# Splits of the first y rows one expert step later, those of the next rows in two items, and double decodings in the odd items

## The chip, the cores and the metric

One NeuronCore of one Trainium2 chip runs the whole program. The time is the device time of one execution in microseconds (us); three runs of the kernel before are shown, and one further execution was profiled. The engines are TensorE (PE, with its weight loads as PEld), VectorE (DVE), ScalarE (ACT), GpSimd (POOL) and SyncE (SP), which here mainly issues DMAs.

## What is computed

Three layers follow each other: causal attention with a bias, a mixture of eight experts that sends each token to one expert, and a gated layer without routing. The change lies at the seam of the last two.

```python
# attention: 4 batches, 8 heads, 576 positions, head size 64
scores = scale * q @ k.T ; bias = min(-(cum_i - cum_j), 0) ; causal
x = softmax(scores + bias) @ v                     # 2304 tokens x 512
# experts: w1 512x1024, w2 1024x512, one of eight for each token
for e in range(8):
    h = np.maximum(x[mask] @ w1[e], 0.0)
    out[mask] = gate_w[mask, None] * (h @ w2[e])
# gated layer: w_a, w_b 512x1536, w_out 1536x512
out = (x @ w_a) * (x @ w_b) @ w_out
```

## The kernel before

**Precision by splitting.** Every matmul operand is held as a hi part and a lo part (hi is the value rounded to a shorter format, lo the rest), and each product takes three matmuls: hi by hi, lo by hi and hi by lo. So each operand costs a cast for hi, mostly on ACT, and a subtraction for lo, on DVE or POOL. In the rows, xh and xl, hh and hl are such pairs, and so are the two halves of a weight tile w, v or u.

**Weights of the gated layer.** They arrive as 64-bit numbers and have to be decoded. `vload` issues the DMA of half a weight into one of three staging buffers (st). `vsplit` decodes one half: ACT scales one word into cv (line 238), DVE shifts the other (239) and merges twice (246, 249). `vfinish` then makes hi on ACT (1207) and lo on POOL (1209) for the half that was decoded one step earlier. A **tick** is one `vload` and one `vsplit`. There are two cv buffers. 36 halves are needed in all: for each pair f, f+1 of twelve column groups a tile of w_a, one of w_b and one of w_out.

**Experts.** `hmm(e, f)` computes column group f (0 to 7) of the hidden layer, 12 matmuls into a PSUM bank h, from which ACT takes hh (1271) and DVE hl (1272). `ymm(e, f)` multiplies the group of one step earlier with w2, 12 matmuls into four banks y. After f = 7 the four y banks are copied to mx tiles (171, 173) and stored to the tensor yt in DRAM (1294), in rows sorted by expert.

**Gated layer.** Rows of yt are processed in six groups i of 384. `yload(i)` loads a group from yt into the one xg buffer (1305). `ysplit(i, d)`, d from 0 to 3, makes hi and lo of a quarter of it: xh on ACT (1312), then xl on DVE (1313). `abmm(i, f)` computes a = y w_a into bank h (12 matmuls, over d) and b = y w_b into bank x (12 more). ACT copies a into an mx tile (1331), DVE multiplies it with b (1333), ACT and DVE make hi and lo of the product (1334, 1335). For i < 2 bank h0 and bank x0 are single, so the next item's a waits for the copy and its b for the product. `omm` (nine matmuls of 512 columns, line 1343) follows one item later.

**Order.** In this part the order on each engine is the order in which the code is written. The last expert, e = 7, runs f = 0 to 7 with one tick in each step. Then come the items, numbered k from 0: (0,0), (0,1), (1,0), (1,1), and from there alternately i = 0 and 1 up to f = 11, item 23; after it groups 2 to 5, without ticks. In items 16 to 20 four small indirect DMAs each, `m6` on POOL (1248), write row numbers and weights to the tensor pm; they are loaded as pmt (1500) before the first output. `oout` scales an output bank by pmt (1352 on ACT, 1354 on DVE) and scatters it by an indirect DMA on POOL (1355).

Of the kernel before, what the change touches and what calls it, by code (L numbers as in the profile page):

```python
# [24 lines left out]
E = 8  # L25
# [7 lines left out]
TICKS = (1, 1, 2)  # L33
# [104 lines left out]
def moe_kernel(tc, q, k, v, s, emb, tau, w1, w2, wa, wb, wo, out, dbg=None):  # L138
# [6 lines left out]
    def pool(st, n, b, **kw):  # L145
        return st.enter_context(tc.tile_pool(name=n, bufs=b, **kw))
# [28 lines left out]
    with left, right:  # L175
# [96 lines left out]
        if True:  # L272
# [816 lines left out]
            def bank(nm, n=2):  # L1089
                turn[nm] = turn.get(nm, -1) + 1  # L1090
                return ps.tile([128, 512], F32, name="%s%d" % (nm, turn[nm] % n))
# [37 lines left out]
            def xtr(e, d):  # L1129
                if d == 0:  # L1130
                    xhs[e] = [xhp.tile([128, 4, GT], F32R, name=x)[:, :, :CAPS[e]] for x in ("xh", "xl")]
                xh, xl = xhs[e]
                cap = CAPS[e]
                pt = bank("x") if e else bank("y", 4)
                for a in range(3):
                    m = min(128, cap - 128 * a)
                    nc.tensor.transpose(  # L1137
                        out=pt[:, 128 * a:128 * a + m], in_=xgs[e][:m, a, 128 * d:128 * d + 128], identity=ident[:m, :m]
                    )
                nc.scalar.copy(out=xh[:, d, :], in_=pt[:, :cap])  # L1140
                nc.vector.tensor_tensor(out=xl[:, d, :], in0=pt[:, :cap], in1=xh[:, d, :].bitcast(F32), op=ALU.subtract)
# [37 lines left out]
            def vload():  # L1179
                if loaded2[0] < len(jobs2):  # L1180
                    key, h, src, _ = jobs2[loaded2[0]]
                    stg[key, h] = slot_load64(src)
                    loaded2[0] += 1
# [3 lines left out]
            def vsplit():  # L1187

                new = None
                if split2[0] < loaded2[0]:  # L1190
                    key, h, _, nm = jobs2[split2[0]]
                    t = stg.pop((key, h))
                    c = decode1(t)
                    new = (key, h, nm, c, split2[0])
                if half:
                    vfinish()
                if new:
                    decode2(t, c)
                    half.append(new)
                    split2[0] += 1  # L1200
# [57 lines left out]
            def hmm(e, f):  # L1258
                ph = bank("h")
                xh, xl = xhs[e]  # L1260
                k_ = 0
                for d in range(4):
                    w = slots[e, d]
                    for hl, mv in ((0, xh), (0, xl), (1, xh)):
                        nc.tensor.matmul(  # L1265
                            ph[:, :CAPS[e]], lhsT=w[:, hl, 128 * f:128 * f + 128], rhs=mv[:, d, :],
                            start=k_ == 0, stop=k_ == 11,
                        )
                        k_ += 1
                hh, hl_ = (hp.tile([128, GT], F32R, name=x)[:, :CAPS[e]] for x in ("hh", "hl"))  # L1270
                nc.scalar.activation(out=hh, in_=ph[:, :CAPS[e]], func=AF.Relu)
                nc.vector.scalar_tensor_tensor(
                    out=hl_, in0=ph[:, :CAPS[e]], scalar=0.0, in1=hh.bitcast(F32), op0=ALU.max, op1=ALU.subtract
                )
                hs[e, f] = (hh, hl_)

            def ymm(e, f):
                if f == 0:
                    ys[e] = [bank("y", 4) for d in range(4)]
                hh, hl_ = hs.pop((e, f))  # L1280
                w = slots[e, 4 + f // 2]
                c0 = 512 * (f % 2)
                for d in range(4):
                    for k_, (hl, mv) in enumerate(((0, hh), (0, hl_), (1, hh))):
                        nc.tensor.matmul(  # L1285
                            ys[e][d][:, :CAPS[e]], lhsT=w[:, hl, c0 + 128 * d:c0 + 128 * d + 128], rhs=mv,
                            start=f == 0 and k_ == 0, stop=f == 7 and k_ == 2,
                        )
                if f == 7:
                    br = nc.sync.value_load(ci[:1, 0, e:e + 1], min_val=max(0, N * (e - 1) // (E - 1)), max_val=N)  # L1290
                    for d in range(4):
                        yv = mxp.tile([128, 512], F32, name="mx")[:, :CAPS[e]]
                        copy("DA"[d % 2], yv, ys[e][d][:, :CAPS[e]])
                        nc.sync.dma_start(out=yt[:, d, bass.ds(br, CAPS[e])], in_=yv)

            def tick():
                vload()
                vsplit()
# [8 lines left out]
            def ysplit(i, d):  # L1307
                if d == 0:
                    yhs[i] = [xhp.tile([128, 4, GT], F32R, name=x) for x in ("xh", "xl")]
                yh, yl = yhs[i]  # L1310
                t = xgs[E + i][:, d, :]
                nc.scalar.copy(out=yh[:, d, :], in_=t)
                nc.vector.tensor_tensor(out=yl[:, d, :], in0=t, in1=yh[:, d, :].bitcast(F32), op=ALU.subtract)  # L1313
# [120 lines left out]
            for e in range(E):  # L1434
                if e == 1:
                    sched.close()
                    overflow()
                    sched.enter_context(tc.manual_schedule())
                for f in range(8):
                    hmm(e, f)  # L1440
                    if (e, f) == (0, 2):
                        most = nc.values_load(ci[:1, 2, 0:1], min_val=-CAP, max_val=N)
                    if prev:
                        ymm(*prev)
                    prev = (e, f)
                    if (e, f) == (0, 1):
                        xload(1)
                    if (e, f) == (1, 0) or f == 7 and 0 < e < E - 2:
                        xload(e + 2 - (f == 0))
                    if (e, f) == (E - 1, 1):  # L1450
                        yload(0)
                    if f == 4 and e + 2 < E:
                        zfill(e + 2)
                    if 3 <= f < 7:
                        if e + 1 < E:
                            xtr(e + 1, f - 3)
                        else:
                            ysplit(0, f - 3)
                    if e == E - 1 and f == 7:
                        yload(1)  # L1460
                    for _ in range(2 if (e, f) == (0, 1) else 1):
                        wsplit2()
                        wload2()
                    if e == E - 2 and f >= 6:
                        vload()
                    if e == E - 1:
                        for _ in range(TICKS[0]):
                            tick()
                    if misc and (e or f > 1):
                        misc.pop(0)()  # L1470

# [3 lines left out]
            for k_, (i, f) in enumerate(items):  # L1475
                abmm(i, f)
                if (i, f) == (NG - 1, 11):
                    for t, x in ((0, 10), (1, 10), (0, 11), (1, 11), (2, 10), (2, 11)):
                        omm1(i, x, t)
                        if x == 11:  # L1480
                            oout(i, t)
                elif k_:
                    omm(*prev)
                else:
                    for d in range(4):
                        ysplit(1, d)
                    ymm(*prev)
                    mo.close()
                    rto.close()
                    rings["u"] = pool(right, "ringc", 1, side="right")  # L1490
                prev = (i, f)
                for _ in range(TICKS[1] + (k_ % TICKS[2] == 0) if i < 2 else 0):
                    tick()
                if (i, f) == (1, 0):
                    yload(2)
                if 16 <= k_ < 21:
                    for t in range(4 * (k_ - 16), 4 * (k_ - 15)):
                        m6(t)
                if k_ == 21:
                    nc.sync.dma_start(out=pmt, in_=pm.rearrange("(t p) x -> p t x", p=128))  # L1500
                if (i, f) == (0, 11):
                    for d in range(4):
                        ysplit(2, d)
                if 1 < i < NG - 1:
                    if f == 1:
                        yload(i + 1)
                    if 4 <= f < 8:
                        ysplit(i + 1, f - 4)
# [34 lines left out]
```

## Time and profile before

| | us |
|---|---|
| runs shown | 986.53, 985.0, 986.75 (median 986.53) |
| profiled execution | 984.46 |
| its span | 982.5 |
| PE busy in it | 950.0 |
| DVE, ACT, POOL busy | 500.9, 425.4, 341.6 |

The span is the stretch that the profile covers; the 1.96 us between it and the execution's time lie outside the trace. Times in the rows below count from the span's start. The last expert runs from about 494 to 519, item 0 starts at 519.1 and item 24 at about 670. A busy time is summed over stages with different limits, so what a part of the code costs is read from the waits and the timeline of its stage.

### The profile page before, as it was taken

The numbers are of one execution on the slowest core, as the hardware profiler recorded it, in microseconds if no ns is written. First come the engines' busy times: TensorE is split into PE (matmuls) and PEld (weight loads), VectorE is DVE, ScalarE is ACT, GpSimd is POOL, SyncE is SP. The second block draws the span as 40 slices with busy tenths as digits, with TensorE's granted clock in tenths as the row PEclk, the third lists the DMA queues.
The fourth block names the chain that finished last, engine by engine and source line by source line (L and its number), as shares of the span: only waits on it lengthen the run. The fifth ranks groups of instructions, "written<-read, shape, count | busy, mean of one in ns | idle before, by whom it ended". The sixth has DMA issues, their size and how long they took to land.

```text
span 982.5 us, 17967 instructions
## 1 busy us (share of the span) xinstructions
PE 950.0 (97%) x6470; PEld 860.2 (88%) x6471; DVE 500.9 (51%) x1312; ACT 425.4 (43%) x1059; POOL 341.6 (35%) x488
## 2 busy tenths in 40 slices
PE   8999999999799999999999999999999999999996
PEld 6787777877589999999999999999999999999995
DVE  5678778787656334444478888723222222222111
ACT  4678777777645444454545444422111111111111
POOL 6665657569423333333333433562001001001001
PEclk8999999999899999999999999999999999999999
DMA  6877897887276766677565544303010010000000
GB/s 169 196 179 194 204 215 195 199 199 210 71 221 174 216 196 211 180 218 217 175 198 180 174 128 127 89 2 98 1 33 33 1 33 33 1 1 33 1 1 32
DMA packets 105413, 123.68 MB, mean 126 GB/s; under 512 B 56937, under 2 KB 71225, under 8 KB 105321
## 3 DMA queue, kind: packets, MB, share of 16 engines
q1 hardware_dynamic: 101433, 112.77, 42.2%
q0 software_dynamic: 3616, 9.48, 2.8%
q8 instruction: 52, 0.85, 0.4%
q14 instruction: 40, 0.33, 0.1%
q10 hardware_dynamic: 272, 0.26, 0.1%
HBM read 86.04 MB, written 19.92 MB: 108 GB/s over the span
## 4 chain that ended last, share of the span: by engine, by line
issue 32%; PE 27%; DVE 3%; POOL 3%; DMA 2%; ACT 0%; POOLq 0%; SPq 0%; DVEq 0%; ACTq 0%
PE h L1265 9%; PE y L1285 9%; PE h L1325 3%; PE x L1325 3%; PE y L1343 2%; POOL out_dram L1355 1%; DMA pm<-pd,pos 1%; DVE cv L246 1%; POOL pm L1248 1%; DVE cv L249 1%; PE x L1137 1%; DMA st<-in_moe_w_b_dram 1%; PE x L1343 0%; PE h L1343 0%; DVE xl L1313 0%
## 5 line engine op out<-in xcount | busy, mean ns | idle before, releaser
L1333 DVE TENSOR_TENSOR mx<-x,mx 128x384 f32<-128x384 f32 x72 | 40.0, 555 | 228.8 <-PE x L1325 228.7
L1355 POOL DMA_INDIRECT out_dram<-mx,pmt x18 | 17.7, 984 | 292.2 <-DVE mx L1354 288.5
L599 ACT ACTIVATE z<-z,mn 128x576 f32<-128x576 f32 (+4 forms) x160 | 89.6, 560 | 48.9 <-DVE mn L593 47.9
L1334 ACT CAST hh<-mx 128x384 fp32r<-128x384 f32 x72 | 36.9, 512 | 163.4 <-DVE mx L1333 163.4
L523 POOL TENSOR_SCALAR bt<-ck,cumc 128x576 f32<-128x576 f32 (+4 forms) x160 | 83.5, 532 | 62.5 <-DMA ck<-cumd 32.5
L1331 ACT COPY mx<-h 128x384 f32<-128x384 f32 x72 | 34.5, 479 | 150.6 <-PE h L1325 150.6
L1325 PE MATMUL h<-xh,w 128*128 128x384 f32 x288 | 79.9, 338 | 1.2 <-ACT mx L1331 0.6
L1325 PE MATMUL h<-xh,v 128*128 128x384 f32 x288 | 79.7, 337 | 0.0
L1325 PE MATMUL x<-xh,w 128*128 128x384 f32 x288 | 79.0, 335 | 0.0
L593 DVE CUSTOM_DVE_ANT_0 z<-st,bt 128x288 f32<-128x288 f32 (+4 forms) x160 | 65.4, 425 | 24.0 <-PE st L582 18.6
L686 PE MATMUL xa<-pT,vn 128*64 128x128 f32 (+1 forms) x960 | 73.4, 280 | 2.8 <-ACT pT L173 1.7
L579 PE MATMUL st<-KS,QS 128*128 128x288 f32 (+4 forms) x192 | 68.7, 366 | 4.0 <-DVE mn L593 2.3
L264 POOL TENSOR_TENSOR w<-st,w 128x512 fp32r<-128x512 f32 (+1 forms) x41 | 44.1, 1084 | 76.2 <-ACT w L256 60.7
L643 PE MATMUL pt<-ident,z 128*128 128x128 f32 (+1 forms) x480 | 69.0, 276 | 0.7 <-DVE x L779 0.4
L686 PEld LDWEIGHTS xa<-pT,vn 128*64 128x64 f32 (+1 forms) x960 | 50.4, 136 | 20.9 <-ACT pT L173 6.0
L264 POOL TENSOR_TENSOR v<-st,v 128x512 fp32r<-128x512 f32 x32 | 42.8, 1339 | 72.0 <-ACT v L256 64.7
L1335 DVE TENSOR_TENSOR hl<-mx,hh 128x384 fp32r<-128x384 f32 x72 | 41.7, 579 | 41.7 <-ACT hh L1334 41.7
L1265 PE MATMUL h<-xh,w 128*128 128x352 f32 (+3 forms) x256 | 62.9, 315 | 0.0
L643 PEld LDWEIGHTS pt<-ident,z 128*128 128x128 f32 (+1 forms) x480 | 51.6, 139 | 12.2 <-issue 6.8
L1265 PE MATMUL h<-xh,v 128*128 128x368 f32 (+3 forms) x256 | 62.0, 313 | 0.0
L1285 PE MATMUL y<-hh,w 128*128 128x352 f32 (+3 forms) x256 | 61.6, 309 | 0.1
L1285 PE MATMUL y<-hh,v 128*128 128x368 f32 (+3 forms) x256 | 60.8, 309 | 0.0
(254 smaller groups left out, 2516.3 us busy)
## 6 DMA issues: line engine op xcount, KB each, us to landing
st<-in_moe_w_dram SPq DMA_DIRECT2D x64, 512.0 KB, 4.3
ck<-cumd SPq DMA_DIRECT2D x16, 576.0 KB, 5.6
QS<-sp SPq DMA_DIRECT2D x56, 144.0 KB, 6.1
st<-in_moe_w_a_dram SPq DMA_DIRECT2D x12, 512.0 KB, 3.7
st<-in_moe_w_b_dram SPq DMA_DIRECT2D x12, 512.0 KB, 4.0
st<-in_moe_w_out_dram SPq DMA_DIRECT2D x12, 512.0 KB, 3.7
xg<-yt SPq DMA_DIRECT2D x6, 768.0 KB, 4.8
xg<-xs SPq DMA_DIRECT2D x8, 512.0 KB, 4.4
```

What stands on the lines that cost most here:

```text
L264: e.tensor_tensor(out=o[:, 1, a:b], in0=t[:, a:b], in1=o[:, 0, a:b].bitcast(F32), op=ALU.subtract)
L523: nc.gpsimd.tensor_scalar(out=bt[:m, h, :kk], in0=cks[u][:m, h, :kk], scalar1=-1.0, scalar2=cumc[:m, c, hh:hh + 1], op0=ALU.mult, op1=ALU.add,
L579: nc.tensor.matmul(st[:m, :wp], lhsT=qs[:, h, s0:s0 + m], rhs=ks[:, h, c0:c0 + wp], start=True, stop=False)
L593: nc.vector.tensor_tensor_reduce(out=z[:m, h, c0:c0 + w], in0=st[:m, :w], in1=bt[:m, h, c0:c0 + w], op0=ALU.add, op1=ALU.min, scale=1.0, s ...
L599: nc.scalar.activation(out=z[:m, h, :kk], in_=z[:m, h, :kk], func=AF.Exp, scale=-1.0, bias=m1, accum_out=rsum[:m, tid(b, c), 2 * p + h:2 * ...
L643: nc.tensor.transpose(out=pt[:m, 128 * x:128 * x + m], in_=z[:m, h, a0:a0 + m], identity=ident[:m, :m])
L686: nc.tensor.matmul(xa[64 * h:64 * h + 64, :m], lhsT=natt["vn", b, 0, bk][:m, 2 * p + h, :], rhs=locs[i][bk, h], start=bk == 0, stop=bk == c,)
L1265: nc.tensor.matmul(ph[:, :CAPS[e]], lhsT=w[:, hl, 128 * f:128 * f + 128], rhs=mv[:, d, :], start=k_ == 0, stop=k_ == 11,)
L1285: nc.tensor.matmul(ys[e][d][:, :CAPS[e]], lhsT=w[:, hl, c0 + 128 * d:c0 + 128 * d + 128], rhs=mv, start=f == 0 and k_ == 0, stop=f == 7 an ...
L1325: nc.tensor.matmul(p, lhsT=w[:, hl, d, c0:c0 + 128], rhs=mv[:, d, :], start=d == 0 and k_ == 0, stop=d == 3 and k_ == 2,)
L1333: nc.vector.tensor_tensor(out=g, in0=pp[1], in1=g, op=ALU.mult)
L1335: nc.vector.tensor_tensor(out=gl, in0=g, in1=gh.bitcast(F32), op=ALU.subtract)
```

## The change

Three things move, and no operation is added or taken away. The four splits of group 0 go from steps f = 3 to 6 of the last expert, ahead of the tick, to f = 4 to 7, behind the tick. The four splits of group 1 go from item 0, ahead of the last `ymm`, to items 0 and 1, two in each, behind the `ymm` or `omm`. And of items 0 to 23 the odd ones now hold two ticks and the even ones one, where it was the other way round.

```diff
-                    if 3 <= f < 7:
-                        if e + 1 < E:
-                            xtr(e + 1, f - 3)
-                        else:
-                            ysplit(0, f - 3)
+                    if 3 <= f < 7 and e + 1 < E:
+                        xtr(e + 1, f - 3)
...
                     if e == E - 1:
                         for _ in range(TICKS[0]):
                             tick()
+                        if f > 3:
+                            ysplit(0, f - 4)
...
                 else:
-                    for d in range(4):
-                        ysplit(1, d)
                     ymm(*prev)
...
                 prev = (i, f)
-                for _ in range(TICKS[1] + (k_ % TICKS[2] == 0) if i < 2 else 0):
+                if k_ < 2:
+                    ysplit(1, 2 * k_)
+                    ysplit(1, 2 * k_ + 1)
+                for _ in range(TICKS[1] + (k_ % TICKS[2] > 0) if i < 2 else 0):
                     tick()
```

`TICKS` is (1, 1, 2). `yload(1)` is issued in f = 7 in both; it writes the xg buffer that all four splits of group 0 read, so it waits for the last of them.

On DVE, the end of the last expert in the order before: `hl<-h_8090` and `hl<-h_8130` belong to f = 6 and f = 7, `xl` is a split of group 0, lines 239 to 249 are a decode, and `mx<-x_8186` is the product of item 0.

```order
L1272 SCALAR_TENSOR_TENSOR hl<-h_8090,hh 128x272
L1313 TENSOR_TENSOR xl<-xg,xh 128x384
L239 TENSOR_SCALAR st_8040<-st_8040 128x512
L246 SCALAR_TENSOR_TENSOR cv<-cv,st_8040 128x512
L249 SCALAR_TENSOR_TENSOR cv<-st_8040,cv 128x512
L1272 SCALAR_TENSOR_TENSOR hl<-h_8130,hh 128x272
L239 TENSOR_SCALAR st_8080<-st_8080 128x512
L246 SCALAR_TENSOR_TENSOR cv<-cv,st_8080 128x512
L249 SCALAR_TENSOR_TENSOR cv<-st_8080,cv 128x512
L1333 TENSOR_TENSOR mx<-x_8186,mx 128x384
```

The same place now:

```order
L1272 SCALAR_TENSOR_TENSOR hl<-h_8088,hh 128x272
L239 TENSOR_SCALAR st_8034<-st_8034 128x512
L246 SCALAR_TENSOR_TENSOR cv<-cv,st_8034 128x512
L249 SCALAR_TENSOR_TENSOR cv<-st_8034,cv 128x512
L1313 TENSOR_TENSOR xl<-xg,xh 128x384
L1272 SCALAR_TENSOR_TENSOR hl<-h_8128,hh 128x272
L239 TENSOR_SCALAR st_8076<-st_8076 128x512
L246 SCALAR_TENSOR_TENSOR cv<-cv,st_8076 128x512
L249 SCALAR_TENSOR_TENSOR cv<-st_8076,cv 128x512
L1313 TENSOR_TENSOR xl<-xg,xh 128x384
L1333 TENSOR_TENSOR mx<-x_8186,mx 128x384
```

The last split stood ahead of the decode of f = 6 and now stands behind that of f = 7, right ahead of item 0's product.

On ACT, from the product of item 0 (`hh<-mx`) to the copy of a in item 1 (`mx<-h_8271` before, `mx<-h_8257` now), before:

```order
L1334 CAST hh<-mx 128x384
L1312 CAST xh<-xg 128x384 x4
L173 COPY mx<-y_7901 128x272
L173 COPY mx<-y_7903 128x272
L238 ACTIVATE cv<-st_8121 128x512
L1207 CAST w_8166<-cv 128x512
L238 ACTIVATE cv<-st_8161 128x512
L1207 CAST w_8266<-cv 128x512
L1331 COPY mx<-h_8271 128x384
```

And now:

```order
L1334 CAST hh<-mx 128x384
L173 COPY mx<-y_7901 128x272
L173 COPY mx<-y_7903 128x272
L1312 CAST xh<-xg 128x384 x2
L238 ACTIVATE cv<-st_8117 128x512
L1207 CAST w_8164<-cv 128x512
L1331 COPY mx<-h_8257 128x384
L1334 CAST hh<-mx 128x384
L1312 CAST xh<-xg 128x384 x2
L238 ACTIVATE cv<-st_8159 128x512
```

Two of the four splits and one of the two decodes now stand behind the copy of item 1.

On POOL, items 16 to 20, where the last lo subtractions (v, u) and the writes to pm stand; before:

```order
L1209 TENSOR_TENSOR v_9113<-cv,v_9113 128x512 x2
L1209 TENSOR_TENSOR u_9174<-cv,u_9174 128x512
L1248 DMA pm<-pd,pos 2304x2 x4
L1209 TENSOR_TENSOR u_9174<-cv,u_9174 128x512
L1248 DMA pm<-pd,pos 2304x2 x4
L1209 TENSOR_TENSOR u_9297<-cv,u_9297 128x512 x2
L1248 DMA pm<-pd,pos 2304x2 x12
```

And now:

```order
L1209 TENSOR_TENSOR v_9113<-cv,v_9113 128x512 x2
L1248 DMA pm<-pd,pos 2304x2 x4
L1209 TENSOR_TENSOR u_9228<-cv,u_9228 128x512 x2
L1248 DMA pm<-pd,pos 2304x2 x4
L1209 TENSOR_TENSOR u_9297<-cv,u_9297 128x512
L1248 DMA pm<-pd,pos 2304x2 x4
L1209 TENSOR_TENSOR u_9297<-cv,u_9297 128x512
L1248 DMA pm<-pd,pos 2304x2 x8
```

The first writes stand one subtraction earlier, and the last subtraction one item later.

## Rows read from the trace of the kernel before

**Rows 1.** The page: busy us, share of the span, count.

```profile
PE 950.0 (97%) x6470; PEld 860.2 (88%) x6471; DVE 500.9 (51%) x1312; ACT 425.4 (43%) x1059; POOL 341.6 (35%) x488
```

**Rows 2.** Waits of PE, 470 to 680 us: total, times, longest.

```profile
PE y L1285 <- DVE hl L1272: 1.6, 1, 1.6
PE h L1325 <- ACT mx L1331: 0.6, 1, 0.6
PE h L1325 <- ACT mx L1352: 0.5, 1, 0.5
```

**Rows 3.** Chain of waits, 500 to 545 us: start, us, what.

```profile
498.86 7.54 DMA st<-in_moe_w_b_dram
...
531.32 0.48 ACT mx L1331
531.85 2.36 PE h L1325 x12
```

**Rows 4.** Timeline of PE, last expert: start, us, instruction [idle before <-releaser].

```profile
510.07 0.39 PE L1285 MATMUL y<-hl,v 128*128 128x272 f32 x1 [1.65 <-DVE hl L1272]
...
514.59 0.29 PE L1285 MATMUL y<-hh,v 128*128 128x272 f32 x1
...
516.10 0.29 PE L1265 MATMUL h<-xh,v 128*128 128x272 f32 x1
```

**Rows 5.** Busy by stretch: PE, PEld, DVE, ACT, POOL, granted clock, DMA share, GB/s.

```profile
510.60:514.10 3.50, 3.50 (x18) 3.50 (x18) 3.36 (x6) 1.73 (x4) 1.44 (x2) 0.51 0.50 150
514.10:519.10 5.00, 5.00 (x41) 5.00 (x41) 4.76 (x7) 2.50 (x5) 3.00 (x2) 1.00 0.57 141
311.60:313.75 2.15, 0.06 (x1) 0.03 (x1) 1.42 (x3) 0.96 (x2) 1.11 (x1) 1.00 0.01 4
313.75:316.00 2.25, 2.25 (x14) 2.25 (x15) 0.77 (x2) 1.14 (x3) 0.16 (x1) 1.00 0.27 87
```

**Rows 6.** Timeline of DVE, last expert and item 0.

```profile
505.66 0.56 DVE L1313 TENSOR_TENSOR xl<-xg,xh 128x384 fp32r<-128x384 f32 x1 [1.13 <-ACT xh L1312]
...
507.21 0.69 DVE L246 SCALAR_TENSOR_TENSOR cv<-cv,st 128x512 uint32<-128x512 uint32 x1 [0.35 <-ACT cv L238]
507.94 1.73 DVE L249 SCALAR_TENSOR_TENSOR cv<-st,cv 128x512 uint32<-128x512 uint32 x1
509.58 0.43 DVE L1272 SCALAR_TENSOR_TENSOR hl<-h,hh 128x272 fp32r<-128x272 f32 x1
...
521.23 1.84 DVE L246 SCALAR_TENSOR_TENSOR cv<-cv,st 128x512 uint32<-128x512 uint32 x1
523.11 0.69 DVE L249 SCALAR_TENSOR_TENSOR cv<-st,cv 128x512 uint32<-128x512 uint32 x1
...
525.32 1.96 DVE L1313 TENSOR_TENSOR xl<-xg,xh 128x384 fp32r<-128x384 f32 x4
```

**Rows 7.** Timeline of ACT, last expert.

```profile
506.48 0.69 ACT L238 ACTIVATE cv<-st 128x512 f32<-128x512 f32 x1 [0.85 <-DMA st<-in_moe_w_b_dram]
```

**Rows 8.** Timeline of PE, items 0 and 1.

```profile
520.84 0.33 PE L1325 MATMUL h<-xl,w 128*128 128x384 f32 x1
521.02 0.33 PE L1325 MATMUL h<-xh,w 128*128 128x384 f32 x1
...
530.81 0.40 PE L1343 MATMUL y<-w,hl 128*128 128x512 f32 x1
```

**Rows 9.** Timeline of SP's queue, the load of rows 384 to 767.

```profile
517.68 0.58 SPq L1305 DMA_DIRECT2D xg<-yt  x1
```

**Rows 10.** Timeline of POOL, items 16 to 20.

```profile
626.62 1.72 POOL L1209 TENSOR_TENSOR v<-cv,v 128x512 fp32r<-128x512 f32 x1 [3.52 <-ACT v L1207]
...
631.35 1.19 POOL L1248 DMA_INDIRECT pm<-pd,pos  x1 [0.16 <-issue]
...
658.95 0.98 POOL L1248 DMA_INDIRECT pm<-pd,pos  x1 [0.30 <-issue]
```

**Rows 11.** Timeline of ACT, the first output copy.

```profile
671.08 0.69 ACT L1352 ACTIVATE mx<-y,pmt 128x512 f32<-128x512 f32 x1 [1.76 <-DMA pmt<-pm]
```

## The prediction

> **What bounds the kernel now.** I read the busy table first: TensorE (PE) is busy 97% of the span [rows 1], so time is lost only where PE waits or runs at a lower clock. Next the waits of PE around the stages that the change touches: from 470 to 680 us there are only three, 1.65 us for DVE's hl in expert 7, 0.64 us for ScalarE's (ACT's) mx copy in item 2, and 0.54 us for an output copy [rows 2]. Then the chain of waits from 500 to 545 us. It enters with a weight DMA that lands at 506.4, runs through DVE step after step, and reaches PE at 531.85 through an ACT copy [rows 3]. So in this stretch DVE has no slack, while PE has some. Last the timelines of PE, DVE, ACT and POOL there, and the granted clock.
>
> The timeline explains the 1.65 us. PE needs hl of f=4, which DVE starts at 509.58 and ends 0.43 later; PE goes on at 510.07, 0.06 after that [rows 4, 6]. DVE stands behind the decode of f=3, whose ACT part began at 506.48 after waiting 0.85 us for the weight DMA [rows 7]. The clock then falls: in the 3.5 us after 510.6 the granted clock is 0.51, that is 1.2 GHz, and from 514.1 on it is 1.00 again [rows 5].
>
> **The change part by part.**
>
> *(A) The first splits one step later.* Before, split (0,0) ran in f=3: DVE did it at 505.66, in time in which it was waiting for the DMA anyway [rows 6]. ACT's half was also done before the DMA landed, since ACT idled 0.85 us after it [rows 7]. So moving it takes nothing out of the way of hl of f=4: the 1.65 us wait stays, and its low clock with it. What the move does is put split (0,d) behind the decode of step f=d+4. For d=3 that is the decode of f=7, whose last DVE operation starts at 523.11 and takes 0.69, ending at 523.80 [rows 6]. From 506.4 to there DVE has one short gap, 0.35 us at 507.21 [rows 6]. The operations up to split (0,3) in the new order are the ones that ended at 523.80, with split (0,0) added, which no longer hides in the DMA wait. A split costs 0.49 (four take 1.96, rows 6). So split (0,3) ends at 523.80 + 0.49 = 524.29, and with the 0.06 PE can use it at 524.35. PE's first matmul on it, in item 0, ran at 520.84 [rows 8]. **Term A: 524.35 - 520.84 = +3.5 us**, of which about 3 us are idle time. The bounds are 3.2 to 3.8: POOL's subtractions hold up a DVE step in each decode (1.73 and 1.84 us against 0.69, rows 6), and with the moved splits between them I let them differ by 0.3, a third of one such hold-up.
>
> The other splits have cover. They stand one f step apart, and a step takes DVE some 3.6 us (the decode of f=3 ended ahead of 509.58, that of f=7 at 523.80, so 14.2 for four; rows 6). So (0,2) ends at about 520.7, some 0.4 late, which the wait for (0,3) swallows, and (0,0) and (0,1) are ready. No hl moves by more than a split's 0.5, and none but that of f=4 was waited for.
>
> *(B) The clock after the new wait.* After the 1.65 us wait PE had 23 matmuls left of the two groups that ended at 514.59; at the pace of the next group, 12 in 1.51 us, they take 2.89, and they took 4.52 [rows 4]. The loss is 1.6 us. The new wait is nearly twice as long, so I take the same: **term B: +1.6 us**. The lower bound is nothing: earlier in the program PE was busy for only 0.06 of 2.15 us, and a clock of 1.00 followed [rows 5]. The upper bound is 1.8, all of 3.5 us at half speed. I take the end of the row that lies in the same stage.
> The Trainium skill (TensorE: Matmul & The Clock Gate, section "Why this matters for your kernels") advises only against idle gaps longer than any forecast here, so by it the clock would hold and term B would be nothing. The trace disagrees, since 1.65 us was enough here [rows 4, 5].
>
> *(C) Item 1's splits in two items, and one decode instead of two in item 0.* Before, the ACT copy that frees PSUM bank h0 for item 2 stood behind four xh casts, two copies and two decodes with their casts; it ran at 531.32, and PE idled 0.64 [rows 2, 3]. From PE's last matmul before it, at 530.81 [rows 8], to 531.85 is 1.04, where two 512-column matmuls follow each other after an estimated 0.23 (0.18 for 384 columns, rows 8, times 512/384), so 0.8 was lost. Now two casts and one decode less stand ahead of the copy, and PE is later, so the wait goes: **term C: -0.8 us**. What is late next is split (1,3), now behind item 1's products. With PE 5 us later, item 2 asks for it 3.8 us after item 1's last matmul (omm's nine at 0.23, then ten of 384 columns at 0.17, an estimate from the same row), and DVE needs some 3.6 for the rest of a decode, the product and its lo part, and two splits. That is near enough that C can shrink to nothing or turn into +0.5.
>
> *(D) Decode parity and the tail on POOL.* From item 2 on each pair of items holds the same three decodes, and each weight is finished in the same or the next item, at least two items ahead of its use. PE waited for none of this between 532 and 676. Only POOL's queue around items 16 to 19 differs: the order shows the last two u subtractions apart, with 8 pm writes behind the last and not 12 behind the pair. POOL has 28.6 us of uninterrupted work from the first pm write, at 631.35, to the end of the 19th, at 658.95 + 0.98 [rows 10]. Now the writes start right behind the last v subtraction. That one ended at 626.62 + 1.72 = 628.34 [rows 10]; it now stands in a single decode behind an item with two, about 1.1 later, so I put the first write at 629.5. One more u subtraction lies inside (1.5, an estimate a little under the v's 1.72), and POOL idles for about 1.3 between the two u of item 17, because only two cv buffers exist and ACT's conversion (0.69, as in rows 7) and its cast wait for POOL's first. 629.5 + 28.6 + 1.5 + 1.3 = 660.9 against 659.93, measured against PE's own place. The pmt load waits for these writes, and ACT's output copy waited 1.76 us for pmt [rows 11], which is what PE's 0.54 at 677 comes from. **Term D: +1.0 us.** The bounds are -0.4 (no idle time on POOL) and +2.6 (a wait of 1.5 there also lowers the clock by 1.6).
>
> Sum: 3.5 + 1.6 - 0.8 + 1.0 = **+5.3 us**. The profiled execution took 984.46 (span 982.5), which is 2.07 under the median of the runs shown, 986.53. On the profiled one I expect 989.8; against the median **991.8 us**, 0.5% slower. A measurement of this kernel can tell about 0.2% (2 us) from no change.
>
> **The rivals.**
>
> *The clock holds.* All as above without B, because the new wait is followed by full clock, as the wait near 313 us was [rows 5]: +3.7, 990.2. The row of this stage speaks against it [rows 5]. The Trainium skill's page named under (B) speaks for it.
>
> *Item 1's rows come late.* The load of them waits for split (0,3) as reader of the only xg buffer. It was issued at 517.68 [rows 9] and now goes out at about 524.3, 6.6 us later while PE is 5 later; before, its splits did not wait for it. They are now due at about 530.5: PE's 14 remaining matmuls of item 0 end near 528.4 at the low clock, and a product, its pair and two copies follow. If the load takes as long as the weight load that followed the first y load, 7.5 us [rows 3], it lands at 531.8; item 2 then waits 1.3, or 2.9 with a low clock: 993.1 to 994.7.
>
> *DVE gets through sooner, and the kernel is faster.* If the moved splits stand beside POOL's subtractions in place of the decode steps that are held up now, each hold-up that goes saves 1.0 (1.73 less 0.69, rows 6). With the four from f=4 to f=7 gone the new wait is gone (3.5); with the fifth, before hl of f=4, that wait shrinks by 1.0 and its low clock (1.6) goes too: -1.0 - 1.6 - 0.8 + 1.0 = -2.4, 984.1. It decides once four of the five are gone. Against it: POOL starts after ACT's cast, which follows the same DVE steps as before, so its place among them hardly moves.
>
> *Half of that.* Two hold-ups gone: a wait of 1.5 without a lower clock, 1.5 - 0.8 + 1.0 = +1.7, 988.2, no measurable change.
>
> That the change doesn't do what it says I exclude: the order shows every move.
>
> **How the numbers follow.** Forecast 55%, clock holds 18%, late rows 12%, half 9%, faster 6%. The likeliest gives 991.8. The lower end is the forecast's small ends, 3.2 + 0 - 0.8 - 0.4 = +2.0 (988.5), less 1.0 for the spread of the runs shown, whose median could as well have been lower: 987.5. The upper end is the late rows with a low clock, 994.7; what is left out is the faster case, most of the half one, and several large ends at once. Slower by over 0.2% are the first three cases, 85%; within it the half one, 9%; faster 6%.
>
> **What would show it.** In the profile after: a PE wait for DVE's xl (line 1313 of before) of about 3 us ending near 524.4, in item 0; the granted clock near 0.5 behind it; the 1.65 us wait before 510.07 unchanged; no PE wait for ACT's mx copy near item 2; the y load of rows 384 to 767 issued at about 524; ACT's wait for pmt longer by about 1 us, and PE's wait near item 25 about 1.5. The forecast is wrong if PE goes through item 0 without that wait, if DVE's steps beside POOL drop to 0.69, or if PE's wait at 510 goes, which would mean that the split and not the DMA held ACT there.

## The result, and the profile after

The changed kernel took 990.92 us in the median of seven runs (988.45 to 992.85), the kernel before beside it 986.38 (982.21 to 988.47): a ratio of 1.0056, 95% interval 1.0040 to 1.0071, or 5.5 us more. The ratio is an estimate of its own and not the quotient of the two medians, which lie 4.54 us apart. The profiled execution took 989.43 with a span of 987.6; before it was 984.46 and 982.5, so 5.1 us of span are to be found. All lines named in the rows stand ahead of the changed ones and keep their numbers.

PE's waits from 470 to 690 us, to be held against [rows 2]: total, times, longest.

```profile
PE h L1325 <- DVE xl L1313: 2.9, 2, 2.5
PE y L1285 <- DVE hl L1272: 2.1, 3, 1.3
PE h L1325 <- ACT mx L1352: 1.5, 1, 1.5
```

The wait for xl is new. The one for ACT's mx copy of line 1331 is gone. The one for the output copy of line 1352 has grown from 0.54 to 1.50. In place of the one hl wait there are three.

The timeline of PE shows where each stands (start, duration, instruction, idle time before it and who ended it).

```profile
510.16 0.40 PE L1285 MATMUL y<-hl,v 128*128 128x272 f32 x1 [1.30 <-DVE hl L1272]
513.96 0.39 PE L1285 MATMUL y<-hl,v 128*128 128x272 f32 x1 [0.52 <-DVE hl L1272]
517.55 0.39 PE L1285 MATMUL y<-hl,v 128*128 128x272 f32 x1 [0.33 <-DVE hl L1272]
520.80 0.45 PE L1325 MATMUL h<-xl,w 128*128 128x384 f32 x1 [0.37 <-DVE xl L1313]
524.35 0.44 PE L1325 MATMUL h<-xl,w 128*128 128x384 f32 x1 [2.52 <-DVE xl L1313]
...
536.00 0.39 PE L1343 MATMUL y<-w,hl 128*128 128x512 f32 x1
536.24 0.33 PE L1325 MATMUL h<-xh,w 128*128 128x384 f32 x1
...
682.04 0.44 PE L1325 MATMUL h<-xh,w 128*128 128x384 f32 x1 [1.50 <-ACT mx L1352]
```

The last of these stood here in the kernel before:

```profile
677.00 0.44 PE L1325 MATMUL h<-xh,w 128*128 128x384 f32 x1 [0.54 <-ACT mx L1352]
```

The same instructions give a ledger of how late PE is against before, step by step. The letters are the terms of the prediction:

| instruction of PE | before | after | late by | what was added |
|---|---|---|---|---|
| first on hl of f=4 | 510.07 [rows 4] | 510.16 | 0.09 | |
| first on split (0,3) | 520.84 [rows 8] | 524.35 | 3.51 | +3.42: A |
| last product of item 1 | 530.81 [rows 8] | 536.00 | 5.19 | +1.68: B |
| first of item 2 | 531.85 [rows 3] | 536.24 | 4.39 | -0.80: C |
| the one that waits for pmt's output copy | 677.00 | 682.04 | 5.04 | +0.65: D, with -0.31 of other small differences |

What held split (0,3) up is on DVE, as [rows 6] let one expect: the decode of f = 7 (lines 239 to 249) stands right ahead of it.

```profile
520.66 0.43 DVE L1272 SCALAR_TENSOR_TENSOR hl<-h,hh 128x272 fp32r<-128x272 f32 x1
521.01 0.42 DVE L239 TENSOR_SCALAR st<-st 128x512 uint32<-128x512 uint32 x1
521.53 1.57 DVE L246 SCALAR_TENSOR_TENSOR cv<-cv,st 128x512 uint32<-128x512 uint32 x1
523.13 0.69 DVE L249 SCALAR_TENSOR_TENSOR cv<-st,cv 128x512 uint32<-128x512 uint32 x1
523.74 0.55 DVE L1313 TENSOR_TENSOR xl<-xg,xh 128x384 fp32r<-128x384 f32 x1
```

Busy time by stretch (PE, PEld, DVE, ACT, POOL, granted clock, DMA share, GB/s), beside [rows 5]: the clock falls to 0.50, that is 1.2 GHz, right behind the new wait, but stays at 1.00 behind the wait before 510.16.

```profile
510.10:514.10 4.00, 3.42 (x25) 3.20 (x26) 3.86 (x7) 2.70 (x7) 1.54 (x2) 1.00 0.47 131
519.10:524.00 4.90, 2.36 (x11) 1.49 (x9) 4.73 (x8) 1.64 (x3) 1.50 (x1) 1.00 0.16 59
...
526.00:528.20 2.20, 2.20 (x8) 2.20 (x8) 0.00 (x0) 0.00 (x0) 0.00 (x0) 0.50 0.95 321
528.20:531.00 2.80, 2.80 (x20) 2.80 (x20) 1.70 (x4) 1.29 (x4) 0.00 (x0) 0.98 0.52 201
```

At the other end, the tail of pm writes on POOL and the output copy on ACT, to be held against [rows 10, 11]: the two u subtractions are now apart by an idle 1.29 us, the 19th write starts at 664.34 instead of 658.95, and ACT waits 2.73 us for pmt instead of 1.76 with its first output copy.

```profile
641.72 1.30 POOL L1209 TENSOR_TENSOR u<-cv,u 128x512 fp32r<-128x512 f32 x1 [1.29 <-ACT u L1207]
...
664.34 0.99 POOL L1248 DMA_INDIRECT pm<-pd,pos  x1 [0.31 <-issue]
670.82 0.91 POOL L1248 DMA_INDIRECT pm<-pd,pos  x1 [5.49 <-DMA pm<-pd,pos]
```

```profile
676.12 0.69 ACT L1352 ACTIVATE mx<-y,pmt 128x512 f32<-128x512 f32 x1 [2.73 <-DMA pmt<-pm]
```

The copy that PE waits for is ACT's next one. It waits in its turn until a scatter of the first copies has landed. It starts 5.18 us after the first one in both profiles, so what pmt is late by is handed on to PE. Before, then after:

```profile
676.26 0.69 ACT L1352 ACTIVATE mx<-h,pmt 128x512 f32<-128x512 f32 x1 [0.67 <-DMA out_dram<-mx,pmt]
...
681.30 0.69 ACT L1352 ACTIVATE mx<-h,pmt 128x512 f32<-128x512 f32 x1 [1.63 <-DMA out_dram<-mx,pmt]
```

### The profile page after: what moved, and what is told of

Same layout as the page of the kernel before. It is cut to its first block, busy times and chain, and to the rows that moved or that the text cites. A ratio compares the mean times of both kernels' runs of the same rounds, so it can differ in the third digit from the quotient of the medians.

```text
span 987.6 us, 17965 instructions
## 1 busy us (share of the span) xinstructions
PE 952.7 (96%) x6470; PEld 861.4 (87%) x6471; DVE 502.5 (51%) x1312; ACT 425.3 (43%) x1059; POOL 343.9 (35%) x488
## 4 chain that ended last, share of the span: by engine, by line
issue 31%; PE 29%; POOL 3%; DVE 3%; DMA 2%; POOLq 0%; ACT 0%; DVEq 0%; ACTq 0%
PE h L1265 9%; PE y L1285 9%; PE x L1325 4%; PE h L1325 3%; PE y L1343 2%; POOL out_dram L1355 1%; POOL pm L1248 1%; DVE cv L246 1%; DMA pm<-pd,pos 1%; PE x L1137 1%; DVE cv L249 1%; DMA st<-in_moe_w_b_dram 1%; PE x L1343 0%; PE h L1343 0%; DMA pmt<-pm 0%
```

## The experiments

The theory is that of the prediction: the loss is the wait for split (0,3) behind the decode of f = 7 (A), often with a low clock behind it (B), and the later tail of pm writes (D), less the wait of item 2 (C). The rivals: all parts of the change share in the loss; DVE bounds the whole stretch, so that PE meets the delay in any case; the clock is no part of it. The twelve kernels ran four at a time, each four on one chip beside the kernel before, the three groups on three different chips. Every ratio is against the kernel before on the same chip; microseconds are the ratio less one, times that kernel's median, with the 95% interval in brackets; the plain difference of two medians can be up to 1.4 us away from this. Single medians of different groups are not comparable (before had 993.27, 991.41 and 984.91).

**Each part alone, and the order against the decode.** The first kernel has only the first part of the change.

```diff
-                    if 3 <= f < 7:
...
-                            ysplit(0, f - 3)
+                    if 3 <= f < 7 and e + 1 < E:
+                        xtr(e + 1, f - 3)
...
                             tick()
+                        if f > 3:
+                            ysplit(0, f - 4)
```

> Only the first part of the change: the splits of group 0 one step later, behind the step's decode. Theory (the new wait for split (0,3) and the low clock after it make the loss): PE waits for DVE's xl in item 0 until about 524.3, the granted clock is near 0.5 for some 3.5 us behind it, and POOL's pm writes stay where they were: +3.5 + 1.6 = +5.1 us, less up to 0.8 since the wait of item 2 is hidden when PE comes later: +4.3 to +5.1. Rival 1 (each of the parts costs something): under +3. Rival 2 (the clock is not part of it): +2.7 to +3.5.

Measured: 1.0058, +5.8 us [4.0, 7.5]. The timeline of its PE has the wait as it was, and the clock behind it is low:

```profile
528.91 0.69 PE L1325 MATMUL h<-xl,w 128*128 128x384 f32 x1 [2.56 <-DVE xl L1313]
```

```profile
528.80:532.00 3.20, 3.09 (x10) 3.10 (x11) 0.05 (x1) 0.48 (x1) 0.00 (x0) 0.52 0.48 135
```

So the first part by itself brings a loss as large as the whole; rival 1 is out, and the value of rival 2 (up to 3.5) lies below the interval. Part of C shows too: the wait of item 2 is still there with 0.47 us.

The second kernel has the other two parts without the first.

```diff
-                    for d in range(4):
-                        ysplit(1, d)
                     ymm(*prev)
...
+                if k_ < 2:
+                    ysplit(1, 2 * k_)
+                    ysplit(1, 2 * k_ + 1)
-                for _ in range(TICKS[1] + (k_ % TICKS[2] == 0) if i < 2 else 0):
+                for _ in range(TICKS[1] + (k_ % TICKS[2] > 0) if i < 2 else 0):
```

> The other two parts without the first: group 1's splits in two items, the double decodings in the odd items. Theory: no PE wait for xl; the wait of item 2 for ACT's mx copy goes (-0.8), PE's wait for the output copy near item 25 grows by 1.0: +0.2 us, no change that can be measured, and 0.8 faster at best. Rival (these parts carry a good share of the loss, through the splits that now stand behind a product or through fewer decodes in item 0): +2 us or more, with a PE wait between 525 and 560 that the kernel before hasn't.

Measured: 1.0002, +0.2 us [-1.3, 1.7]: no change, as the theory says. But the profile holds a surprise. From 470 to 700 us PE waits for the following:

```profile
PE h L1325 <- ACT mx L1352: 4.5, 1, 4.5
PE y L1285 <- DVE hl L1272: 2.2, 3, 1.6
```

The wait for the output copy is 4.5 us here, where the changed kernel's profile had 1.50, and with the first part alone on the same chip it is 2.49. The item-2 wait is gone. So D is not the same in every execution; the last two groups follow this up.

The third kernel is the changed one with the split of group 0 ahead of the step's tick.

```diff
+                        if f > 3:
+                            ysplit(0, f - 4)
                         for _ in range(TICKS[0]):
                             tick()
-                        if f > 3:
-                            ysplit(0, f - 4)
```

> The changed kernel with one thing turned round: in steps f=4 to f=7 of the last expert the split of group 0 stands ahead of the step's decode and not behind it; it still comes one step later than in the kernel before. Theory (what costs is that split (0,3) stands behind the decode of f=7): split (0,3) ends near 521 and PE has no wait of over 0.5 us for it, so terms A and B go and +0.2 to +1.0 us against the kernel before is left, 4 to 5 us less than the changed kernel. Rival (DVE is the bound of the whole stretch, and PE would meet the same delay at the next thing it needs from DVE): +3 us or more, with a wait for DVE's hl or mx of 2 us in its place.

Measured: 1.0017, +1.7 us [0.1, 3.3], with these waits of PE:

```profile
PE h L1325 <- ACT mx L1352: 4.1, 1, 4.1
PE y L1285 <- DVE hl L1272: 1.6, 1, 1.6
PE h L1325 <- DVE xl L1313: 0.3, 1, 0.3
```

Of the wait for xl 0.34 us is left, and nothing of its size took its place in that stretch. From PE's first matmul on hl of f = 4 to the one on split (0,3) it is 11.25 us here (515.54 to 526.79), against 14.19 in the changed kernel and 10.77 before. It is the decode in front that costs, not the later step; the rival (3 or more) has only the top 0.3 us of the interval, and its wait is not there. The value is above the expected +0.2 to +1.0, on a chip where D is large.

**The clock.** The fourth kernel fills the wait with work whose result is overwritten.

```diff
...
                         for k_, (hl, mv) in enumerate(((0, yh), (0, yl), (1, yh))):
+                            if (i, f, nm, d, k_) == (0, 0, "a", 3, 1):
+                                warm(first[1], w[:, 0, 0, c0:c0 + 128], yh[:, 0, :], 12)
                             nc.tensor.matmul(
...
```

`warm` issues 12 matmuls into bank x0, which item 0's b overwrites later; the lines left out take that bank earlier.

> The changed kernel with 12 matmuls of 384 columns more, which write a PSUM bank that is overwritten afterwards, put into PE's queue in item 0 right ahead of the first matmul that needs split (0,3). They take some 2.2 us, less than the wait, and need nothing that is late. Theory (the low clock is a consequence of PE standing still): the matmul that waits runs at about 524.35 as in the changed kernel, the clock stays at 1.00 behind it, and the kernel is 1.6 us less than the changed kernel, +3.9 against the kernel before. Rival 1 (the clock falls for another reason): the 0.5 stays behind 524 and the time is that of the changed kernel, +5.5. Rival 2 (the added work only costs): +7.

Measured: 1.0062, +6.2 us [4.9, 7.4]: no gain over the changed kernel's +5.5 is seen, and the expected +3.9 lies below the interval. Yet the timeline and the clock did what the theory said:

```profile
525.78 2.25 PE L167 MATMUL x<-xh,w 128*128 128x384 f32 x12
528.49 0.44 PE L1332 MATMUL h<-xl,w 128*128 128x384 f32 x1 [0.47 <-DVE xl L1313]
```

```profile
524.00:528.50 4.50, 3.66 (x20) 2.73 (x18) 4.30 (x7) 1.03 (x2) 1.53 (x1) 1.00 0.01 4
528.50:532.00 3.50, 3.50 (x22) 3.50 (x23) 0.56 (x1) 0.57 (x2) 0.00 (x0) 1.00 0.59 171
```

The 12 matmuls take 2.25 us, the wait shrinks to 0.47 and the clock stays at 1.00. (Lines 1325 and 1352 have the numbers 1332 and 1359 in this kernel.) On that chip, though, PE then waited 3.80 us for the output copy, and such a wait can take back what PE wins ahead of it. So the eighth kernel repeats the test with the pm writes out of the way.

**The changed kernel on a second chip, and the pm writes.** The fifth is the changed kernel itself.

> The changed kernel once more, beside the three that follow. In the runs so far the wait for pmt at item 25 was 2.5 us with the first part alone and 3.8 to 4.5 with the double decodings moved, where the first profile of the changed kernel had 1.50. Theory (its length hangs on how soon the last pm writes land, and that differs between chips): a wait for xl of 2.5 us again and a wait for pmt of 1.5 or of about 4 us, +5.5 us with the one and +7 to +9 with the other. Rival (the wait near 681 costs nothing in the end): +5.5 in both cases.

Measured: 1.0056, +5.6 us [3.5, 7.6]; the rival gave the right time. Its profile has both waits, and a clock that behaves the other way round:

```profile
529.26 0.45 PE L1325 MATMUL h<-xl,w 128*128 128x384 f32 x1 [2.53 <-DVE xl L1313]
...
687.17 0.45 PE L1325 MATMUL h<-xh,w 128*128 128x384 f32 x1 [3.27 <-ACT mx L1352]
```

```profile
529.20:532.00 2.80, 2.74 (x16) 2.75 (x17) 0.00 (x1) 0.48 (x1) 0.00 (x0) 1.00 0.42 103
...
688.00:691.00 3.00, 3.00 (x11) 3.00 (x11) 0.48 (x1) 0.27 (x1) 1.60 (x2) 0.50 0.61 231
```

The same instructions, a wait of 2.53 us against 2.52, and this time full clock behind it. The low clock comes behind the wait for pmt instead. With the writes in their old order PE waited 2.49 us for pmt as well (first kernel), so the kernel before probably has a longer wait on such chips too, and the ratio stays the same; it was not profiled there.

The sixth is the kernel before with the pm writes spread over earlier items.

```diff
-                if 16 <= k_ < 21:
-                    for t in range(4 * (k_ - 16), 4 * (k_ - 15)):
+                if 8 <= k_ < 18:
+                    for t in range(2 * (k_ - 8), 2 * (k_ - 7)):
                         m6(t)
```

> The kernel before with one thing changed: the twenty pm writes stand two behind each of items 8 to 17, not four behind each of items 16 to 20, so that they end some 16 us sooner. Theory (PE's wait near 677 comes from the tail of pm writes on GpSimd): the wait goes, -0.5 us where it was 0.5, and -2.5 to -4 where it was 2.5 with a lower clock behind it. Rival (the writes hold up subtractions, and with them the weights): new PE waits for u or v between 580 and 640, no gain or a loss.

Measured: 0.9981, -1.9 us [-3.5, -0.4], between the two values expected. The wait is gone: ACT's first output copy now follows PE at once.

```profile
676.69 0.69 ACT L1352 ACTIVATE mx<-y,pmt 128x512 f32<-128x512 f32 x1 [0.22 <-PE y L1343]
```

The seventh is the changed kernel with the same edit.

> The changed kernel with the pm writes moved in the same way. Theory: term D is gone, A, B and C stay: a wait for xl of 2.5 us in item 0 with a low clock behind it, none for pmt; against the kernel with early pm writes alone +4.3 us (3.5 + 1.6 - 0.8), against the changed kernel -1.5 to -4 by the length of its wait. Rival (D was not the writes but the parity's later weights): the wait near 681 stays.

Measured: 1.0014, +1.4 us [-0.6, 3.5]; that is 4.2 less than the changed kernel beside it, and 3.3 more than the sixth, where 4.3 was expected. The wait near 681 is gone, and the rival with it. A, B and the wait at 510 are all in its profile (2.55 us for split (0,3), then 0.52 of the clock). In this execution PE also waited 1.18 us at 636.35 for an ACT copy that stood behind a decode waiting 4.45 us for its weight DMA. The sixth has no such wait, and neither have the eighth and the tenth, which have the same writes and double decodings in the same items; so these don't bring it every time, and its cause stays open.

The eighth is the filled kernel with early pm writes.

> The changed kernel with early pm writes and the 12 added matmuls ahead of the one that waits for split (0,3), so that nothing near 681 covers what they do. Theory (the low clock follows from PE's idle time): clock 1.00 behind 524, 1.6 us less than the changed kernel with early pm writes alone. Rival (the clock's loss is given back later, or the filling costs as much): the same time as that kernel, within 0.5.

Measured: 1.0007, +0.7 us [-0.6, 1.9], that is 0.7 less than the seventh, with intervals of some 2 us: the time decides nothing between 1.6 and 0. In the profile the clock is 1.00 behind the filled wait. The fifth kernel had a full clock without any filling, so a full clock in two filled profiles doesn't show that the filling keeps it.

What a low clock costs in this stretch can be read from the profiles themselves, from the matmul on split (0,3) to PE's first of item 2. In the five below PE does the same work and has no wait on the way; the first kernel is left out, since it waits for item 2.

| profile | split (0,3) | first of item 2 | between | clock behind the wait |
|---|---|---|---|---|
| changed kernel, first | 524.35 | 536.24 | 11.89 | 0.50 |
| seventh | 529.08 | 540.95 | 11.87 | 0.50 |
| changed kernel, fifth | 529.26 | 539.57 | 10.31 | 1.00 |
| fourth, filled | 528.49 | 538.83 | 10.34 | 1.00 |
| eighth, filled | 526.69 | 537.00 | 10.31 | 1.00 |

So one fall of the clock costs PE 1.5 to 1.6 us here, also between two profiles of the same kernel. Over many executions the mean granted clock of each timed one gives a second look. It is 0.9874 on average in the sixth kernel, 0.9857 in the seventh and 0.9867 in the eighth (12 executions each). The 0.0017 between the sixth and the seventh are, as an estimate over 990 us, 1.7 us of full clock, give or take 1.5 (two standard errors): the clock has a share in the loss. The eighth can't be told from either.

**The parity, both causes together, and a kernel that is faster than both.** The ninth has the third part alone (the last two lines of the second kernel's diff).

> Only the third part of the change: the double decodings in the odd items. Theory (this part moves the tail of pm writes back against PE's place by 1 us): no wait for xl; PE's wait for the output copy at item 25 is about 1 us longer than with the first part alone, where it was 2.5, with a low clock behind it; the wait for ACT's mx copy at item 2 may go; +0.2 to +1.0 us. Rival (the part carries most of the loss on this chip, since early pm writes took 4 us from the changed kernel and 1.9 from the kernel before): +2 us.

Measured: 1.0007, +0.7 us [-0.5, 1.9]. The rival (+2) is out, if only just, and nothing clear of zero is left. The wait for the output copy is 2.48 us with a clock of 0.50 behind it; how long it is in the kernel before, or with the first part alone, on this chip was not seen, so that it grows by 1 us is not shown here.

The tenth joins the third and the seventh: splits ahead of the decode, writes early.

> The changed kernel with both suspected causes taken away: the splits of group 0 ahead of the decode, and the pm writes early. Theory (the loss is the wait for split (0,3) plus the wait for pmt, and the two add): as fast as the kernel before with early pm writes, 0.998, or up to 0.8 us less by term C. Taken from the runs: 5.5 less 3.8 (what the first alone took) less 4.1 (what the second took) = -2.4 us. Rival (they overlap, or a third cost is left): +0 or more.

Measured: 0.9989, -1.1 us [-2.8, 0.5], between theory and rival. The two large waits are gone; what is left in its profile is the old hl wait (1.57 us, with full clock behind it) and small ones of 0.29 to 0.65.

The eleventh is the kernel before with early pm writes and no tick in step f = 3 of the last expert, the decode that waits for its weight DMA [rows 7].

```diff
-                        for _ in range(TICKS[0]):
+                        for _ in range(0 if f == 3 else TICKS[0]):
                             tick()
```

> The kernel before with early pm writes and without the decode step of f=3 in the last expert (the 36 units need 37 steps, and 44 are there; the later steps take over). Theory (the wait for DVE's hl of f=4 comes from that decode, which waits for its weight DMA): the wait of 1.6 us and its low clock go, 2 to 3 us less than early pm writes alone: 0.995 to 0.996. Rival (with a full clock PE catches up with DVE and waits at f=5 to 7 in small pieces, as it did where the clock held): 1 us or less, 0.997 to 0.998.

Measured: 0.9974, -2.6 us [-4.0, -1.2]. The hl wait is gone altogether and the clock stays at 1.00 there. Of PE's waits from 470 to 700 us one is left:

```profile
PE h L1325 <- ACT mx L1331: 1.0, 1, 1.0
```

The time lies in the rival's band, the mechanism was the theory's: the wait went, but against the sixth kernel, on another chip, the gain is only 0.7, with intervals so wide that 2 us are not excluded.

The twelfth has in addition the second and third part of the change, while group 0's splits stay where they were.

> The kernel before with the second and third part of the change, early pm writes and without the decode step of f=3 in the last expert; group 0's splits stay where they were. Theory: as the kernel before it without those parts, less up to 0.8 us by the wait of item 2: 0.994 to 0.996. Rival (with one decode step fewer and double decodings in odd items a weight comes late): a PE wait for v or u between 540 and 640, and no gain.

Measured: 0.9967, -3.2 us [-4.8, -1.8], median 980.36 against 984.91. From 470 to 700 us PE waits once:

```profile
PE h L1325 <- DVE xl L1313: 0.2, 1, 0.2
```

The rival's wait for a weight between 540 and 640 is not there. The twelfth kernel is faster than the kernel before, and by that than the changed one. Two of the three parts of the change are in it; what it leaves out is the first. Its interval overlaps with that of the eleventh beside it, so what these two parts bring can't be told from nothing.

## Why the prediction was right

990.92 against a forecast of 991.8, and the range held it. By its steps:

- **A, +3.5.** The matmul on split (0,3) was put at 524.35 and started at 524.35; the ledger gives 3.42. The first kernel shows that this part alone brings a loss of that size, the third that turning the split and the decode round takes the wait away. The step that carried it was to count DVE's operations as one unbroken chain from the weight DMA on. It holds in every profile with this order: from PE's matmul on hl of f = 4 to the one on split (0,3) it is 14.19 us in after, 14.21 with the first part alone (514.70 to 528.91), 14.21 in the fifth kernel (515.05 to 529.26), and 14.20 to 14.24 in the fourth, seventh and eighth, whether PE ran at half or full clock in between. The prediction had 14.28.
- **B, +1.6.** 1.68 in the profile that was compared, and 1.58 between two profiles of the changed kernel. So the size was right, but that the clock would fall was put too firmly. Of four profiles with this wait unfilled, at 2.52 to 2.56 us, three show the low clock and one does not. Held against the rival "the clock holds", which was given 18%, both happen, and with the same kernel. That the profile compared was one of those with the low clock was luck; with the clock held its ledger would have ended 1.6 us lower. The Trainium skill (TensorE: Matmul & The Clock Gate, section "Why this matters for your kernels") advises only against longer idle gaps than these, so by it the clock would hold each time; the trace disagrees, with 0.50 behind 2.52 us.
- **The wait before 510.** Predicted to stay with its low clock. It stayed with 1.30 us and the clock held. That should have made PE 1.6 us earlier; it didn't, since PE then waited for DVE at each following step (0.52, 0.33, 0.37) and met the same end at 524.35. So the sentence that no hl but that of f = 4 is waited for was wrong too. Both misses cost nothing because DVE, not PE, set that end. In the order before it is nearly so as well: from hl of f = 4 to split (0,3) PE took 10.77 us in the kernel before and 10.78 in the ninth, with a low clock, and 10.41 in the second and 10.44 in the sixth, at full clock. Of the 1.6 us that the low clock takes from PE there, only some 0.35 is left.
- **C, -0.8.** -0.80 in the ledger; the copy that item 2 needs was no longer late, and split (1,3) was not late either.
- **D, +1.0.** The wait grew by 0.96, from 0.54 to 1.50. ACT's longer wait for pmt was put at 1.0 and was 0.97. The 19th write was put to end at 660.9 against PE's place and ended at 660.94 (664.34 + 0.99, less the 4.39 by which PE was late at item 2). The third part alone measured +0.7 [-0.5, 1.9], which is not clear of zero; with early writes the wait is gone. What the prediction did not know is how much longer this wait is on other chips. On the second one early writes took 4.2 us from the changed kernel and 1.9 from the kernel before, so that D comes to 2.3 there and A, B and C together to 3.3, each to within 2 or 3 us only: much the same sum, perhaps from other shares.
- **Late rows.** Their load went out at 524.32, as forecast, and item 2 did not wait for it.

```profile
524.32 0.57 SPq L1305 DMA_DIRECT2D xg<-yt  x1
```

- **DVE through sooner.** The hold-ups beside POOL stayed, one in each step: line 246 took 1.81, 1.61, 1.61 and 1.57 us in the steps f = 4 to 7, where the last had 1.84 before [rows 6]; at 507.30, where POOL's subtraction began only after it (507.91), it took 0.69.

## What to carry to other kernels

A step that is put behind another on an in-order engine waits for all that stands in front, so count the operations from the last true idle time of that engine to the new place and compare the end with the first use. When a producer is the bound of a stretch, losses and gains of the consumer inside that stretch cancel at the next hand-over: judge a moved step at the hand-over, not at the waits in between. And a small wait that hangs on a chain of DMA writes should be given room, since its length can differ between chips: 1.50 and 3.27 us in the two profiles of the changed kernel.

## What the hardware showed beyond that

The clock behind an idle PE is not the same from execution to execution. After hl waits of 1.57 to 1.65 us it fell to 0.50 in six profiles (the kernel before, the first part alone, the third, seventh, eighth and ninth kernels). It held at 1.00 in two, the tenth kernel and the second, whose row behind a wait of 1.62 us is this:

```profile
516.00:520.00 4.00, 3.67 (x28) 3.45 (x29) 3.86 (x7) 2.41 (x7) 1.71 (x2) 1.00 0.45 131
```

The 20th pm write waits for an earlier one to land before POOL can start it: 5.92 and 5.49 us in the first pair of profiles, 7.36 to 8.01 on the chip of the first four kernels, 7.08 on the next and 6.49 on the third. PE's wait for the output copy grows with it. In the six profiles with late writes and the double decodings in the odd items it is 1.50, 2.48, 3.27, 3.80, 4.13 and 4.50 us, where the 20th write waited 5.49, 6.49, 7.08, 7.52, 7.80 and 8.01. The row below is that of the second kernel, the longest.

```profile
674.00 0.91 POOL L1248 DMA_INDIRECT pm<-pd,pos  x1 [8.01 <-DMA pm<-pd,pos]
```
